# The last two groups' first FFN product made jointly by Strassen's seven block products

## The chip, the core and the metric

The kernel runs on one core of a Trainium2 chip. The metric is the device time of one execution in microseconds (us), the median over several runs. The engines of the core are TensorE (PE, matrix products into PSUM), VectorE (DVE), ScalarE (ACT), GpSimd (POOL) and SyncE (SP, which issues DMAs). In the profile PEld is TensorE's weight load, which runs beside its products.

## What is computed

Attention with squared ReLU scores for 8 batches, 12 heads, 448 rows of 64, then a Fourier mix, a normalisation and a feed-forward network (FFN) over the 3584 rows of 768:

```
scores = 1/8 * q @ k^T ; attn = relu(scores)^2 / 448 ; x = attn @ v      # heads side by side: 768 columns
u  = x + real(fft(fft(x, axis=rows), axis=columns))
un = (u - mean(u)) / sqrt(var(u) + 1e-6)                                 # over the 768 columns
out = u + relu(un @ w_ch1) @ w_ch2                                       # 768 -> 3072 -> 768
```

Only the last line concerns the change: `un @ w_ch1` is the first product, `h @ w_ch2` the second.

## The kernel before

The rows of the FFN are cut into 12 groups by `GT`: 384, 512 and 384 rows, then nine groups (numbers 3 to 11) of 256. A group's normalised rows stand transposed in SBUF as `unT`, six blocks of 128 columns of the model by up to 512 rows. Groups 2 and up get it through DRAM: `turns` issues transposing DMAs on SP (L1160) into two homes that alternate between odd and even groups, so group 11's transposes wait until TensorE has read group 9's.

**First product (`ffn`, L1446 to L1461).** For each of the 24 blocks `j` of 128 hidden columns there are six matmuls (over `m`, weights `w1_sb[m][hf]`, 128x128 each, loaded at once into SBUF), with 256 moving columns. Two blocks share one PSUM bank of the pool `BF` (two banks, `psF`), then one Relu on ACT or DVE (`relu`, L1409) writes 128x512 in bf16 to `hT`, the home of the hidden layer.

**Second product.** For groups of 256 rows it is already done by Strassen's scheme: class `Pair` takes two 128-row halves L and R of the group, even and odd blocks of the hidden layer as the inner halves, and the two column halves of `w_ch2` (384 each). `early` forms sums of hidden blocks on DVE (L1565 to L1569) in three pieces `CH` of 6, 4 and 2 block pairs, `late` one more (L1577), and `chain_a` and `chain_b` run seven products of 12 matmuls (L1583, 384 moving columns), in which a bank goes on accumulating after DVE has added what it holds so far to an output tile (`add`, L1438). The sums of the weights `T[1]` to `T[4]` are formed once, by `weight_sums` on DVE. SP loads `u` into the output tiles `o0` to `o5` and stores them (`outputs`, L1370 and L1374).

**What sets the order.** The kernel writes its own program order. Everything is a generator ("stream") that yields `need(engine, duration, deps, bufs)` and issues its instructions when it is resumed; `Streams.run` always resumes the stream whose next step could start first by its own cost estimates, with a rank to break ties:

```
LATENCY = {"PE": 0.28, "ACT": 0.18, "DVE": 0.16, "POOL": 0.2, "SP": 0.1}
def mm(n):   return n / 2400 + 0.006
def act(n):  return n / 1200 + 0.2
def dve(n):  return n / 960 + 0.15
```

`Bufs` and `Banks` are the planner's own books on which buffers are free. The real waits (semaphores) are put in by the tile framework from the tiles that instructions read and write, in the order written. PSUM has eight banks: three tiles `psS` of two banks (pool `BS`, `[128, 2, 512]` in f32, used for scores) and two tiles `psF` of one (`BF`). Each engine runs its instructions in order.

**Around the last groups.** Attention and the mix of the last batch end at about 475 us; from there on TensorE only runs FFN groups, one after the other: first product of 144 matmuls, second of 84, group 8 from 461.8 us, 9 from 491.2, 10 from 520.6, 11 from 549.9. `ffns` (L1378) runs the groups in turn.

Of the kernel before, what the change touches and what calls it, by code (L numbers as in the profile page):

```python
# [9 lines left out]
FP32 = mybir.dt.float32  # L10
# [154 lines left out]
def kernel(  # L165
# [488 lines left out]
        BX[m].free.append(e)  # L654
        x_ready[b][m].t = e

    chains = [0]

    def attention(b, left=None):

# [8 lines left out]
        while pa < NB:  # L669
# [38 lines left out]
            for part in ("scores", "values") if few else ("values", "scores"):  # L708
                if part == "values" and values:
                    held = homes.take()  # L710
                    av = held[:, 0] if homes is BS else held
                    give = lambda when, homes=homes, held=held: homes.give(held, when)
                    vn, h0 = loads[bv * NG + mv // 2][2], 2 * mv % HG
                    for c in range(4):
                        sq, _, at = sv.pop(4 * mv + c)
                        sq_ids.append((e, at))
                        for h in range(2):
                            nc.tensor.matmul(av[h * Dh:(h + 1) * Dh, 0:S], lhsT=vn[:, c, h0 + h, :],  # L718
                                             rhs=sq[:, h, :], start=(c == 0), stop=(c == 3))
                        BSQ.free.append(e)  # L720
                    av_end = e - (n * mm(S) + SWITCH if n and not few else 0.0) + LATENCY["PE"]
                    if mv % 2 == 1:
                        BQ[2].free.append(e)
                    if left is None:
# [651 lines left out]
            yield need("SP", 0.0, [e])  # L1376

    def ffns():  # L1378
        for b in range(NGR):
            yield need("SP", 0.0, [group_ready[b]])  # L1380
            yield from ffn(b)

    def ffn(b):
        T0, N, unT = groups[b]
# [24 lines left out]
        def relu(ph, e, j):  # L1409
# [18 lines left out]
            for x in ht[j:j + JN]:  # L1428
                x.t = e + LATENCY["ACT"]

        left = {(c, hf): 1 + (b > 0 and hf == 1 if c in WHOLES[b] else (c % 2, hf) != (0, 1))
                for c in range(NC) for hf in range(2)}

        def add(pc, e, c, hf, give=True):

            e = yield need("DVE", dve(DH), [e + LATENCY["PE"], ot[b, c, hf]])
            o = os[b, c, hf]
            nc.vector.tensor_tensor(o, pc[:, 0:DH], o, op=ALU.add)  # L1438
            if give:
                BF.give(pc, e)  # L1440
            left[c, hf] -= 1
            if not left[c, hf]:
                added[b, c, hf].t = e + LATENCY["DVE"]
            return e + LATENCY["DVE"]

        for j in range(0, JC, JN):  # L1446
            hf, jj = divmod(j, JC // 2)
            e = yield need("PE", 6 * JN * mm(N), [w1_ready[hf]] + ([group_ready[b]] if b > 1 else []), [BF])
            ph = BF.take()
            for i in range(JN):  # L1450
                for m in range(MC):
                    nc.tensor.matmul(ph[:, i * N:(i + 1) * N], lhsT=w1_sb[m][hf][:, (jj + i) * 128:(jj + i + 1) * 128],  # L1452
                                     rhs=unT[:, m, 0:N], start=(m == 0), stop=(m == MC - 1))
            advance(6 * JN * mm(N))
            sch.add(relu(ph, e, j), (0, 0))
            if j == JC // 2:
                ffn_begun[b].t = e
                pairs = [Pair(b, c, h, ht, add, advance) for c in PAIRS[b]]
                for p in pairs:
                    sch.add(p.early(), (0, 0.3))  # L1460
                    sch.add(p.late(), (0, 0.3))  # L1461
        if b == 0:
            unt_left.t = e
        else:
            BUNT.free.extend([e, e] if b == 2 else [e])

        for c in WHOLES[b]:
            if b > 0:
# [67 lines left out]
    class Pair:  # L1536
# [1 line left out]

        read = []

        def __init__(self, b, c, h, ht, add, advance):
            self.b, self.c, self.h, self.ht, self.add, self.advance = b, c, h, ht, add, advance
            self.L, self.R = slice(c * 128, c * 128 + 128), slice(c * 128 + 128, c * 128 + 256)
            self.ev = [slice(2 * i0, 2 * i1, 2) for i0, i1 in CH]
            self.od = [slice(2 * i0 + 1, 2 * i1, 2) for i0, i1 in CH]
            self.r12, self.r4 = ([Cell() for _ in CH] for _ in range(2))
            self.m1, self.m2, self.done = Cell(), Cell(), [Cell(), Cell()]
            self.reads = Cell(), Cell()
            self.waits, Pair.read = Pair.read, [self.reads[0], self.reads[1], *self.r4]

        def early(self):

            h, L, R_ = self.h, self.L, self.R
            if not made:
                yield need("DVE", 0.0, [un_left])
                a1 = work.tile([128, 6, 128], BF16, name="s1", tag="un2", bufs=1)
                a2 = work.tile([128, 6, 128], BF16, name="s2", tag="un3", bufs=1)
                at = JC * 256 + KP * DH
                for a, m in ((a1, upper(at, 6, 128)), (a2, upper(at + 6 * 128, 6, 128))):
                    made.append([a, m[:, 0:4], m[:, 4:6]])  # L1560
            for k, (i0, i1) in enumerate(CH):
                ev, od, s1, s2 = self.ev[k], self.od[k], made[0][k], made[1][k]
                d = dve2((i1 - i0) * 128)
                yield need("DVE", d, self.ht[2 * i0:2 * i1] + self.waits + ([upper_free] if k else []))
                nc.vector.tensor_tensor(s1, h[:, ev, R_], h[:, od, R_], op=ALU.add)  # L1565
                yield need("DVE", d)
                nc.vector.tensor_tensor(s2, s1, h[:, ev, L], op=ALU.subtract)
                e = yield need("DVE", d)
                nc.vector.tensor_tensor(h[:, ev, R_], h[:, ev, L], h[:, ev, R_], op=ALU.subtract)  # L1569
                self.r12[k].t = e + LATENCY["DVE"]  # L1570

        def late(self):

            h, L = self.h, self.L
            for k, (i0, i1) in enumerate(CH):
                e = yield need("DVE", dve2((i1 - i0) * 128), [self.m2, self.r12[k]])
                nc.vector.tensor_tensor(h[:, self.od[k], L], h[:, self.od[k], L], made[1][k], op=ALU.subtract)  # L1577
                self.r4[k].t = e + LATENCY["DVE"]

        def product(self, pc, lhs, rhs, start, i0=0, i1=KP):  # L1580

# [5 lines left out]
        def first(self, k):  # L1587

            cut = KP - 3
            yield need("PE", cut * mm(DH), self.ht[k:2 * cut:2] + [self.m1] * k, [BF])  # L1590
            pc = BF.take()
            chains[0] += 1
            self.product(pc, self.block(k, self.L), self.weights(k, 0), True, 0, cut)
            e = yield need("PE", (KP - cut) * mm(DH), self.ht[2 * cut + k::2])
            self.product(pc, self.block(k, self.L), self.weights(k, 0), True, cut)
            return pc, e

        def block(self, k, cols):

            return [self.h[:, 2 * i + k, cols] for i in range(KP)]  # L1600

        def formed(self, n):

            return [made[n][k][:, i - i0] for k, (i0, i1) in enumerate(CH) for i in range(i0, i1)]

        def weights(self, k, hf):

# [23 lines left out]
        def chain_b(self):  # L1631
# [5 lines left out]
            e = yield need("PE", d, [sums[3]] + self.r12, [BF])  # L1637
            pc = BF.take()
# [27 lines left out]
    with tc.manual_schedule():  # L1666
# [50 lines left out]
```

## Time and profile before

| | |
|---|---|
| median of 3 runs | 584.08 us (583.7 to 585.09) |
| the profiled execution, its own time | 584.67 us |
| its span, first to last instruction | 582.8 us |
| granted TensorE clock, mean | 0.997 |
| last matmul issued until | about 579.2 us |
| last output add on DVE | 579.34 to 579.90 us |

Three groups of instructions of the page that touch the change:

| group | count | mean of one |
|---|---|---|
| L1452 matmul, first product, all shapes | 1728 | 291 ns |
| L1583 matmul 128x384, second product, plain weights | 462 | 326 ns |
| L1438 add 128x384 f32 on DVE | 92 | 553 ns |

A matmul's duration in such a row includes the time in the pipeline behind the matmul before it; what a matmul costs TensorE is the distance from start to start. The span is what the profile covers; the own time of the execution is longer by what lies around it.

### The profile page before, as it was taken

Reading aid. Unit: us, or ns where it says so; the run is one execution under the profiler, and the core shown is the slowest. Engines: PE = TensorE matmul, PEld = TensorE weight load, DVE = VectorE, ACT = ScalarE, POOL = GpSimd, SP = SyncE. Lnnn points to the kernel's source line nnn. Section 1 sums busy time; section 2 is a strip of 40 time slices with the busy share of each in tenths; the row PEclk is TensorE's granted clock in tenths of the full one; section 3 lists DMA queues with packets and bytes.
Section 4 is the critical chain, followed back from the end, with each engine's and each line's share of the span. In section 5 each row is a group of like instructions: output and inputs, shape, how many; then the busy total and the mean of one; then the engine's idle time right before and its main releaser. Section 6 shows DMA issues by size and latency. Waiting matters only on the chain.

```text
span 582.8 us, 11457 instructions
## 1 busy us (share of the span) xinstructions
PE 572.9 (98%) x4476; PEld 365.7 (63%) x4476; DVE 406.4 (70%) x927; ACT 335.0 (57%) x511; POOL 133.7 (23%) x188
## 2 busy tenths in 40 slices
PE   8999999999999999999999999999999999999997
PEld 7566556544455546556857667568577786868684
DVE  5978667986669988787787878987946852222222
ACT  5866873587745787676668748777654340304040
POOL 8534021411115313421333032303300230000000
PEclk9998999999999999999999999999999999999999
DMA  9999999776947997699579987993433353031201
GB/s 120 206 211 227 222 210 134 173 131 95 181 57 189 207 172 168 116 216 167 122 123 207 180 153 147 200 176 115 126 75 100 118 151 99 30 94 36 79 30 55
DMA packets 133493, 81.85 MB, mean 140 GB/s; under 512 B 77504, under 2 KB 128704, under 8 KB 133440
## 3 DMA queue, kind: packets, MB, share of 16 engines
q0 software_dynamic: 40320, 33.63, 38.2%
q1 hardware_dynamic: 93120, 47.50, 36.3%
q8 instruction: 35, 0.57, 0.4%
q14 instruction: 18, 0.15, 0.1%
HBM read 62.91 MB, written 26.25 MB: 153 GB/s over the span
## 4 chain that ended last, share of the span: by engine, by line
PE 88%; DVE 6%; ACT 4%; issue 1%; POOL 0%; DVEq 0%; ACTq 0%; POOLq 0%
PE psF L1452 37%; PE psF L1583 26%; PE psS L736 6%; PE psF L718 5%; PE psF L1503 3%; PE psF L1477 3%; PE psS L1212 2%; ACT sq L761 2%; DVE sq L776 2%; PE psS L718 1%; PE psS L823 1%; PE psS L1026 1%; PE psS L1187 1%; PE psF L505 0%; ACT un L1087 0%
## 5 line engine op out<-in xcount | busy, mean ns | idle before, releaser
L1452 PE MATMUL psF<-unT,w 128*128 128x256 bf16 (+2 forms) x1728 | 229.8, 291 | 1.2 <-ACT unT L999 0.9
L1452 PEld LDWEIGHTS <-w 128*128 128x128 bf16 x1728 | 165.9, 98 | 61.6 <-issue 11.5
L761 ACT ACTIVATE sq<-psS 112x896 bf16<-112x896 f32 x192 | 164.4, 918 | 38.4 <-PE psS L736 38.0
L1426 ACT ACTIVATE hT<-psF 128x512 bf16<-128x512 f32 (+3 forms) x169 | 87.9, 532 | 116.6 <-PE psF L1452 115.8
L776 DVE TENSOR_TENSOR sq<-sq 112x896 bf16<-112x896 bf16 x161 | 100.6, 638 | 16.6 <-ACT sq L761 15.6
L1583 PEld LDWEIGHTS <-hT 128*128 128x128 bf16 x792 | 76.0, 98 | 54.4 <-issue 5.8
L1438 DVE TENSOR_TENSOR o<-psF,o 128x384 f32<-128x384 f32 x92 | 50.9, 553 | 44.8 <-PE psF L1583 39.6
L1583 PE MATMUL psF<-w,hT 128*128 128x384 bf16 x462 | 81.7, 326 | 0.3 <-DVE hT L1424 0.2
L736 PE MATMUL psS<-qkT 64*128 64x448 bf16 (+1 forms) x384 | 51.6, 359 | 1.2 <-ACT qkT L510 0.4
L718 PE MATMUL psF<-sq,vn 112*64 112x448 bf16 x320 | 37.9, 358 | 0.3 <-DVE o L1438 0.3
L557 DVE TENSOR_SCALAR xT<-psF 128x224 bf16<-128x224 f32 x58 | 19.8, 383 | 26.3 <-PE psF L718 26.2
L376 POOL DMA_DIRECT2D vn<-in_v_dram x24 | 17.3, 720 | 76.0 <-PE psS L736 67.7
L1059 POOL TENSOR_TENSOR u<-tp,xn 112x385 f32<-112x385 f32 (+2 forms) x14 | 13.3, 953 | 93.1 <-DVE tp L1041 81.5
L1583 PE MATMUL psF<-wsum,hT 128*128 128x384 bf16 x198 | 34.6, 326 | 0.0
L736 PEld LDWEIGHTS <-qkT 64*128 64x128 bf16 (+1 forms) x384 | 15.9, 102 | 28.7 <-issue 21.2
L376 POOL DMA_DIRECT2D qn<-in_q_dram x21 | 15.5, 739 | 69.9 <-DVE qkr L469 49.6
L718 PEld LDWEIGHTS <-vn 112*64 112x64 bf16 x384 | 17.8, 109 | 21.4 <-issue 13.7
L773 ACT ACTIVATE sq<-sq 112x896 bf16<-112x896 bf16 x31 | 29.5, 956 | 0.5
L1068 DVE BATCH_NORM_STATS2 stats<-u 112x6 f32<-112x384 f32 (+2 forms) x56 | 28.4, 541 | 0.0
L1087 ACT ACTIVATE un<-u,nmr,rstd 112x768 bf16<-112x768 f32 (+2 forms) x22 | 22.4, 1025 | 7.3 <-DVE nmr L1074 5.0
L1477 PE MATMUL psF<-w,hT 128*128 128x384 bf16 x144 | 25.1, 326 | 0.0
L1503 PE MATMUL psF<-w,hT 128*128 128x384 bf16 x144 | 24.7, 326 | 0.0
(166 smaller groups left out, 612.6 us busy)
## 6 DMA issues: line engine op xcount, KB each, us to landing
out_dram<-o SPq DMA_DIRECT2D x56, 192.0 KB, 2.2
vn<-in_v_dram POOLq DMA_DIRECT2D x24, 224.0 KB, 5.9
qn<-in_q_dram POOLq DMA_DIRECT2D x21, 224.0 KB, 5.3
kn<-in_k_dram POOLq DMA_DIRECT2D x21, 224.0 KB, 5.5
w<-in_moe_w_ch_dram POOLq DMA_DIRECT2D x12, 384.0 KB, 14.5
w<-in_moe_w_ch_dram POOLq DMA_DIRECT2D x4, 1152.0 KB, 20.5
utop<-u SPq DMA_DIRECT2D x12, 336.0 KB, 3.1
o<-utop SPq DMA_DIRECT2D x16, 192.0 KB, 3.8
```

The source lines that it names most:

```text
L376: nc.gpsimd.dma_start(out=t, in_=src[b, hs].rearrange("h (p j) d -> p h (j d)", j=4))
L718: nc.tensor.matmul(av[h * Dh:(h + 1) * Dh, 0:S], lhsT=vn[:, c, h0 + h, :], rhs=sq[:, h, :], start=(c == 0), stop=(c == 3))
L736: nc.tensor.matmul(sc[:wide, h, 0:S].rearrange("k (c q) -> k c q", c=4), lhsT=flat[ps, k0:k0 + wide], rhs=qT[ps, m % 2], start=True, stop= ...
L761: nc.scalar.activation(r, sc[:R, :, 0:S], AF.Relu)
L773: nc.scalar.activation(r, r, AF.Square)
L776: nc.vector.tensor_tensor(r, r, r, op=ALU.mult)
L1426: nc.scalar.activation(hs, ps, AF.Relu)
L1438: nc.vector.tensor_tensor(o, pc[:, 0:DH], o, op=ALU.add)
L1452: nc.tensor.matmul(ph[:, i * N:(i + 1) * N], lhsT=w1_sb[m][hf][:, (jj + i) * 128:(jj + i + 1) * 128], rhs=unT[:, m, 0:N], start=(m == 0), ...
L1477: nc.tensor.matmul(pc[:, 0:DH], lhsT=block(j, c), rhs=w2(j, hf), start=(j == 0), stop=(j == JC - 1))
L1503: nc.tensor.matmul(pc[:, 0:DH], lhsT=block(2 * i + k, c), rhs=weights[i], start=(start and i == 0), stop=(i == KP - 1), skip_group_check=True)
L1583: nc.tensor.matmul(pc[:, 0:DH], lhsT=lhs[i], rhs=rhs[i], start=(start and i == 0), stop=(i == KP - 1), skip_group_check=True)
```

## The change

Groups 10 and 11 (`ga`, `gb` in the code, `NGR - 2` and `NGR - 1`) no longer run `ffn`. Their first product is made jointly in `last_two`. Write A for group 10's rows and B for group 11's, lo and hi for the first and last three blocks `m` of the inner 768, and even and odd for the hidden blocks. The product of [A; B] with the weights is a product of 2x2 blocks; Strassen's scheme (in Winograd's form) makes it by seven block products in place of eight, with four sums of weights `S_[1..4]` and four differences of inputs `Tk[1..4]`.

- `quarter_sums` is a new stream on DVE. It forms the 24 weight sums of 128x768 (four sums, three `m`, two halves `hf`), in homes that the attention has left: the tiles of the squared scores `sq0` to `sq5`, `qkT`, `qkr`, `xT`, the folds; the third sum overwrites weights in `w1_sb` once group 9's first product is done. Then it forms the four input differences in the tables of the Fourier mix (`chan`) and in `seqm`. It begins once the last attention product is planned (`last_values`).
- `last_two` takes all three `psS` tiles and uses their halves as six banks `B6`, and four sets `BK` of three f32 copies in old homes of the mix (`u`, `qs`, `tp`, `un`, `pc`). For each of 12 rounds `i` (a pair of hidden blocks) `main` runs four products in one bank that goes on accumulating, with a copy on ACT after each of the first three and a Relu on ACT after the last; `second` and `third` run the other three in banks of their own and add a copy on DVE (`sum_out`, with a Relu in place behind it). Even the order of the rounds is left to the planner.
- The hidden layer of group 11 goes to new homes (`hB`, tiles `xn` and `vn`), and its `Pair` runs in the banks `B6`, cut into four pieces, with sums in four of the `quarter` homes. The two `Pair`s are planned together with the joint product.
- `Pair` and the output add (`adder`, moved out of `ffn`) take their pieces, homes and bank pool as arguments; for the other groups they do what they did.

The core of the diff, with the new functions:

```diff
     def ffns():
-        for b in range(NGR):
+        for b in range(NGR - 2):
             yield need("SP", 0.0, [group_ready[b]])
             yield from ffn(b)
+        yield from last_two()
...
+    def w1_part(k, m, hf):
+        return w1_sb[m][hf].rearrange("p (i o c) -> p i o c", o=2, c=128)[:, :, k]
...
+        def form(n, m, hf, x, y, op, deps=(), home=None):
+            e = yield need("DVE", dve2(6 * 128), deps)
+            if home is None:
+                home = homes.pop(0)
+            nc.vector.tensor_tensor(home, x, y, op=op)
...
+                yield from form(1, m, hf, w1_part(1, m, hf), w1_part(1, m + 3, hf), ALU.add)
+                yield from form(2, m, hf, S_[1][m, hf], w1_part(0, m, hf), ALU.subtract)
+                yield from form(4, m, hf, w1_part(0, m + 3, hf), S_[2][m, hf], ALU.subtract)
...
+                yield from form(3, m, hf, w1_part(0, m, hf), w1_part(1, m, hf), ALU.subtract, [ffn1_left],
+                                w1_part(1, m, hf))
...
+        for n, x, y in ((1, lambda: b2[:, lo], lambda: b1[:, lo]), (2, lambda: b2[:, hi], lambda: Tk[1]),
+                        (3, lambda: b2[:, hi], lambda: b2[:, lo]), (4, lambda: b1[:, hi], lambda: Tk[2])):
+            e = yield need("DVE", dve2(768), [group_ready[ga], group_ready[gb]])
+            Tk[n] = homes[n - 1]
+            nc.vector.tensor_tensor(Tk[n], x(), y(), op=ALU.subtract)
...
+    def last_two():
+        ga, gb = NGR - 2, NGR - 1
+        N = 256
+        yield need("PE", 0.0, [group_ready[ga], group_ready[gb]], [BS] * 3)
+        tiles = [BS.take() for _ in range(3)]
+        B6 = Banks(6, lambda i: tiles[i // 2][:, i % 2])
...
+        def product(ps, n, k, i, rhs, start, stop):
+            hf, ii = divmod(i, 6)
+            for m in range(3):
+                lhs = w1_part(n, m + k, hf)[:, ii] if k is not None else S_[n][m, hf][:, ii]
+                nc.tensor.matmul(ps[:, 0:N], lhsT=lhs, rhs=rhs[:, m], start=(start and m == 0),
+                                 stop=(stop and m == 2), skip_group_check=True)
+        d, half_done = 3 * mm(N), Cell()
+        def copy(ps, dst, e):
+            e = yield need("ACT", act(N), [e + LATENCY["PE"]])
+            nc.scalar.copy(dst, ps[:, 0:N])
+            return e + LATENCY["ACT"]
+        def sum_out(q, u, t, dst, deps, done, hta):
+            e = yield need("DVE", dve(N), deps, [BH[t]] if hta is not None else [])
+            nc.vector.tensor_tensor(dst, q[:, 0:N], u, op=ALU.add)
+            done(e)
+            e = yield need("DVE", 0.2)
+            nc.vector.tensor_scalar(dst, dst, 0.0, None, op0=ALU.max)
+            return e + LATENCY["DVE"]
+        def main(i):
...
+            e = yield need("PE", d, [], [B6, BK])
+            p, bk = B6.take(), BK.take()
+            product(p, 0, 0, i, b1[:, 0:3], True, False)
+            sch.add(second(i, m1, cs), (5 + 0.1 * i, 5 + 0.1 * i))
+            m1.t = e = yield from copy(p, cs[0], e)
+            e = yield need("PE", d, [e, QS[2], QT[2]])
+            product(p, 2, None, i, Tk[2], False, False)
+            e = yield from copy(p, cs[1], e)
+            e = yield need("PE", d, [e, QS[1], QT[1]])
+            product(p, 1, None, i, Tk[1], False, False)
...
+            sch.add(third(i, u4, cs, bk), (5 + 0.1 * i, 5 + 0.1 * i))
+            u4.t = e = yield from copy(p, cs[2], e)
+            e = yield need("PE", d, [e, QS[4]])
+            product(p, 4, None, i, b2[:, 3:6], False, True)
+            e = yield need("ACT", act(N), [e + LATENCY["PE"]])
+            nc.scalar.activation(at_b(0, i, i + 1, every)[:, 0], p[:, 0:N], AF.Relu)
...
+        def second(i, m1, cs):
+            e = yield need("PE", d, [], [B6])
+            r = B6.take()
+            product(r, 0, 3, i, b1[:, 3:6], True, True)
+            hta[2 * i].t = yield from sum_out(r, cs[0], 2 * i, at_a(0, i, i + 1, every)[:, 0], [e + LATENCY["PE"], m1],
+                                              lambda e: B6.give(r, e), True)
+        def third(i, u4, cs, bk):
+            e = yield need("PE", d, [QS[3], QT[3]], [B6])
+            q = B6.take()
+            product(q, 3, None, i, Tk[3], True, False)
...
+            e1 = yield need("PE", d, [gone, QT[4]])
+            product(q, 1, 3, i, Tk[4], False, True)
...
+        for i in range(KP):
+            sch.add(main(i), (5 + 0.1 * i, 5 + 0.1 * i))
...
+        pairs = [Pair(ga, 0, at_a, hta, adder(ga, 2, BF), skip, own, BF),
+                 Pair(gb, 0, at_b, htb, adder(gb, 2, B6), skip, cut, B6)]
...
+        sch.add(quarter_sums(), (6, 6))
```

In the built program TensorE has 4440 matmuls where it had 4476, DVE 102 instructions more and ACT 26 more. The order of TensorE's instructions is the same up to the first product of group 10.

More of the change, by code (lines that the diff above doesn't have):

```diff
@@ L1378, in ffns, with adder, add @@
     def ffns():
-        for b in range(NGR):
+        for b in range(NGR - 2):
             yield need("SP", 0.0, [group_ready[b]])
             yield from ffn(b)
+        yield from last_two()
+    def adder(b, NC, pool):
+        left = {(c, hf): 1 + (b > 0 and hf == 1 if c in WHOLES[b] else (c % 2, hf) != (0, 1))
+                for c in range(NC) for hf in range(2)}
+        def add(pc, e, c, hf, give=True):
+            e = yield need("DVE", dve(DH), [e + LATENCY["PE"], ot[b, c, hf]])
+            o = os[b, c, hf]
+            nc.vector.tensor_tensor(o, pc[:, 0:DH], o, op=ALU.add)
+            if give:
+                pool.give(pc, e)
+            left[c, hf] -= 1
+            if not left[c, hf]:
+                added[b, c, hf].t = e + LATENCY["DVE"]
+            return e + LATENCY["DVE"]
+        return add
@@ new lines, in last_two, with at_a, at_b, given @@
+    def last_two():
+        ga, gb = NGR - 2, NGR - 1
+        N = 256
+        yield need("PE", 0.0, [group_ready[ga], group_ready[gb]], [BS] * 3)
+        tiles = [BS.take() for _ in range(3)]
+        B6 = Banks(6, lambda i: tiles[i // 2][:, i % 2])
+        yield need("SP", 0.0, [], BU[0][1:] + BU[1][1:])
+        for x in "", "1":
+            t = work.tile([128, 3, N], FP32, name="copies", tag=f"u{x}B", bufs=1)
+            copies.append([t[:, n] for n in range(3)])
+        yield need("SP", 0.0, [], [BTS, BUN[0]])
+        ones = [work.tile([128, N], FP32, name="copies", tag=t, bufs=1)
+                for t in ("qs", "tp", "un0", "un1", f"pc{TC[0][0]}", f"pc{TC[1][0]}")]
+        copies.extend((ones[0:3], ones[3:6]))
+        BK = Banks(4, lambda i: Set(copies[i]))
+        halves = hid[0].rearrange("p j n -> p (j n)").rearrange("p (x j n) -> p x j n", x=2, n=256)
+        hA = halves[:, 0]
+        b1, b2 = groups[ga][2], groups[gb][2]
+        hta, htb = ([Cell() for _ in range(JC)] for _ in range(2))
+        def at_a(k, i0, i1, cols):
+            return hA[:, 2 * i0 + k:2 * i1:2, cols]
+        def at_b(k, i0, i1, cols):
+            for c0, c1, t in hb:
+                if c0 <= i0 < c1:
+                    assert i1 <= c1
+                    return t[:, 2 * (i0 - c0) + k:2 * (i1 - c0):2, cols]
+        every = slice(0, N)
+        def product(ps, n, k, i, rhs, start, stop):
+            hf, ii = divmod(i, 6)
+            for m in range(3):
+                lhs = w1_part(n, m + k, hf)[:, ii] if k is not None else S_[n][m, hf][:, ii]
[12 more added lines that the diff above has]
+            nc.vector.tensor_scalar(dst, dst, 0.0, None, op0=ALU.max)
+            return e + LATENCY["DVE"]
+        def main(i):
+            m1, u4 = Cell(), Cell()
+            e = yield need("PE", d, [], [B6, BK])
+            p, bk = B6.take(), BK.take()
+            cs = bk.aps
+            product(p, 0, 0, i, b1[:, 0:3], True, False)
[6 more added lines that the diff above has]
+            product(p, 1, None, i, Tk[1], False, False)
+            if i == 5:
+                half_done.t = e + LATENCY["PE"]
+            sch.add(third(i, u4, cs, bk), (5 + 0.1 * i, 5 + 0.1 * i))
[4 more added lines that the diff above has]
+            nc.scalar.activation(at_b(0, i, i + 1, every)[:, 0], p[:, 0:N], AF.Relu)
+            B6.give(p, e)
+            htb[2 * i].t = e + LATENCY["ACT"]
+        def second(i, m1, cs):
[8 more added lines that the diff above has]
+            product(q, 3, None, i, Tk[3], True, False)
+            gone = Cell()
+            def given(e):
+                gone.t = e + LATENCY["DVE"]
+            def first():
+                htb[2 * i + 1].t = yield from sum_out(q, cs[2], None, at_b(1, i, i + 1, every)[:, 0],
+                                                      [e + LATENCY["PE"], u4], given, None)
+            sch.add(first(), (0, 0))
+            e1 = yield need("PE", d, [gone, QT[4]])
+            product(q, 1, 3, i, Tk[4], False, True)
+            def leave(e):
+                B6.give(q, e)
+                BK.give(bk, e)
+            hta[2 * i + 1].t = yield from sum_out(q, cs[1], 2 * i + 1, at_a(1, i, i + 1, every)[:, 0],
+                                                  [e1 + LATENCY["PE"]], leave, True)
+        ffn_begun[ga].t = ffn_begun[gb].t = sch.engine["PE"]
+        for i in range(KP):
+            sch.add(main(i), (5 + 0.1 * i, 5 + 0.1 * i))
+        skip = lambda us: None
+        own = [(k, i0, i1) for k, (i0, i1) in enumerate(CH)]
+        cut = [(k, max(i0, c0), min(i1, c1)) for k, (i0, i1) in enumerate(CH) for c0, c1, _ in hb
+               if max(i0, c0) < min(i1, c1)]
+        pairs = [Pair(ga, 0, at_a, hta, adder(ga, 2, BF), skip, own, BF),
+                 Pair(gb, 0, at_b, htb, adder(gb, 2, B6), skip, cut, B6)]
+        own_sums = [S_[n][m, 0] for n, m in ((1, 0), (1, 1), (2, 0), (2, 1))]
+        pairs[1].waits = [half_done, pairs[0].r12[0]]
+        pairs[1].sums = lambda n, i0, i1: own_sums[2 * n + i0 // 6][:, i0 % 6:i0 % 6 + i1 - i0]
+        for n, p in enumerate(pairs):
+            sch.add(p.early(), (0, 7 + n))
+            sch.add(p.late(), (0, 7 + n))
+            sch.add(p.chain_a(), (7 + 1 * n, 0))
+            sch.add(p.chain_b(), (6.9 + 1 * n, 0))
+        yield need("SP", 0.0, pairs[1].done)
@@ L1429, in relu @@
                 x.t = e + LATENCY["ACT"]
[L1431 to L1444, printed above, removed]
+        add = adder(b, NC, BF)
         for j in range(0, JC, JN):
@@ L1568, in early @@
                 e = yield need("DVE", d)
[L1569 to L1570 removed]
+                nc.vector.tensor_tensor(at(0, i0, i1, R_), at(0, i0, i1, L), at(0, i0, i1, R_), op=ALU.subtract)
+                self.r12[x].t = e + LATENCY["DVE"]
         def late(self):
[L1574 to L1578, printed above, removed]
+            at, L = self.at, self.L
@@ new lines, in late, with sums @@
+            for x, (k, i0, i1) in enumerate(self.pieces):
+                e = yield need("DVE", dve2((i1 - i0) * 128), [self.m2, self.r12[x]])
+                nc.vector.tensor_tensor(at(1, i0, i1, L), at(1, i0, i1, L),
+                                        self.sums(1, i0, i1), op=ALU.subtract)
+                self.r4[x].t = e + LATENCY["DVE"]
+        def sums(self, n, i0, i1):
+            k = [c0 <= i0 < c1 for c0, c1 in CH].index(True)
+            return made[n][k][:, i0 - CH[k][0]:i1 - CH[k][0]]
@@ L1598, in block @@
         def block(self, k, cols):
-            return [self.h[:, 2 * i + k, cols] for i in range(KP)]
+            return [self.at(k, i, i + 1, cols)[:, 0] for i in range(KP)]
         def formed(self, n):
-            return [made[n][k][:, i - i0] for k, (i0, i1) in enumerate(CH) for i in range(i0, i1)]
+            return [self.sums(n, i, i + 1)[:, 0] for i in range(KP)]
         def weights(self, k, hf):
@@ L1636, in chain_b @@
             yield from self.add(pc, e, c, 0)
-            e = yield need("PE", d, [sums[3]] + self.r12, [BF])
-            pc = BF.take()
+            e = yield need("PE", d, [sums[3]] + self.r12, [self.pool])
+            pc = self.pool.take()
             self.product(pc, self.block(0, self.R), T[3], True)
```

77 lines of the change are left out of this document (61 added, 16 removed).

## The prediction

> **What bounds the kernel now.** I read the page's engine table first, then the chain of waits in order of time, then the timeline of the last 120 us engine by engine.
>
> ```profile
> PE 572.9 (98%) x4476; PEld 365.7 (63%) x4476; DVE 406.4 (70%) x927; ACT 335.0 (57%) x511; POOL 133.7 (23%) x188
> ...
> 520.56 15.72 PE psF L1452 x144
> 536.28 13.65 PE psF L1583 x84
> 549.93 15.72 PE psF L1452 x144
> 565.65 13.66 PE psF L1583 x84
> ```
>
> The last two groups are four blocks of TensorE work end to end, with nothing between them. A first-product matmul takes 15.72/144 = 0.1092 us, so one over a 128x256 tile pays 288 x 0.1092 = 31.45 us for the two groups that the change touches. Only TensorE time counts here, and any wait of TensorE is paid in full. The other engines are nearly idle in this stage: the page's 40 slices give DVE 2 tenths in the last seven, ACT 0 to 4.
>
> What one handover costs (TensorE ends, another engine reads PSUM, TensorE goes on) can be read from the timeline:
>
> ```profile
> 520.40 15.88 PE L1452 MATMUL psF<-unT,w 128*128 128x256 bf16 x144
> 521.96 0.60 ACT L1426 ACTIVATE hT<-psF 128x512 bf16<-128x512 f32 x1 [14.35 <-PE psF L1452]
> 477.38 4.06 PE L1583 MATMUL psF<-w,hT 128*128 128x384 bf16 x24
> 479.53 0.56 DVE L1438 TENSOR_TENSOR o<-psF,o 128x384 f32<-128x384 f32 x1 [0.50 <-PE psF L1583]
> 124.51 0.66 ACT L999 CAST unT<-psS 128x582 bf16<-128x582 f32 x1
> 125.22 0.59 PE L1452 MATMUL psF<-unT,w 128*128 128x512 bf16 x2 [0.92 <-ACT unT L999]
> ```
>
> Twelve matmuls from 520.40 are issued by 521.71 and ACT starts at 521.96: 0.25. Twelve of 0.1626 (13.66/84) from 477.38 end at 479.33 and DVE starts at 479.53: 0.20. ACT ends at 125.17 and TensorE starts at 125.22: 0.05. The rows by shape give the reads:
>
> ```profile
> L1426 ACT ACTIVATE hT<-psF 128x256 bf16<-128x256 f32 x18 | 6.9, 385 | 5.4 <-PE psF L1452 5.1
> L1424 DVE TENSOR_SCALAR hT<-psF 128x256 bf16<-128x256 f32 x6 | 2.5, 420 | 1.2 <-PE psF L1452 1.2
> L333 DVE TENSOR_SCALAR channeg<-chan 128x386 bf16<-128x386 bf16 x3 | 0.8, 259 | 0.4 <-ACT chan L310 0.4
> ```
>
> So a handover over ACT is 0.25 + 0.385 + 0.05 = 0.685 us, over DVE 0.20 + 0.42 + 0.05 = 0.67. In the old kernel six matmuls per bank half and twelve per bank (1.31 us) stand between two uses, so nothing is felt.
>
> **The change part by part.**
>
> *Removed:* 288 matmuls (31.45 us, all on the path) and 24 Relus of 128x512 on ACT (0.60 each, beside TensorE).
>
> *Added on TensorE:* 12 rounds of 7 products of 3 matmuls, 252 x 0.1092 = 27.52 us. The gain before any wait is 31.45 - 27.52 = **3.93 us**. The second product's 168 matmuls of 0.1626 stay.
>
> *Added weight sums:* 24 DVE adds of 128x768 and four of the inputs, at the 0.55 of the early sums of the pair (L1565 to L1569, 0.55 to 0.56). Eighteen stand between 448 and 479 us, 18 x 0.47 (step from start to start) = 8.5 us, where DVE's idle times add up to 9.4 (2.65, 0.30, 0.29, 0.85, 0.65, 0.20, 2.73, 1.24, 0.50); also two DVE Relus of 0.69 there go to ACT. They queue ahead of the early sums of group 8's pair, which ended at 479.02 and are needed by the matmul at 481.28: 2.3 us of cover, so nothing. Six more overwrite weights after group 9's last first-product matmul (506.75) and push one output add by about 0.45, needed only at 510.65 and over at 509.9: nothing. The four input differences wait for group 11's transposes, issued at 506.94 and 508.16, landing in at most 3.5 us, ahead of their place in DVE's queue (513.4). TensorE's order up to 520.40 is unchanged in the built program, and no bank wait there was close (0.4 us left at each psF). I take 0 for all of this, bounds 0 and 2 (the overflow of 8.5 over 9.4 if the sums cannot use the small gaps).
>
> *Moved DMAs:* SP's loads of group 11's outputs stand some 30 us earlier; the one that reuses a slot (store of group 10's first block, 2.2 us to landing, then a load, 3.6) is ready about 15 us after the second product begins, when DVE reaches its add. By this estimate DVE waits at most 0.3 there, and behind it stands an add that TensorE releases 1 us later. Zero.
>
> *Added waits, the heart of it.* The joint stage takes the three two-bank psS tiles and uses their halves as six banks. Per round there are four ACT reads and three DVE sums (each with a Relu in place behind it, 0.23 by L333's row). The planner knows a wait only per half. In the built program the waits follow the whole tile: of the 59 waits of TensorE on a psS tile in this stage, 35 are for ACT or DVE reading the *other* half, and ACT and DVE wait for matmuls and for each other across halves too. So a tile is a queue: product, read, product, read. With a product of 3 x 0.1092 = 0.33, the next product in a tile waits 0.68 less 0.33 for each product placed between: 0.68, 0.36 or 0.03 for none, one or two.
>
> I walked the 84 products in the built order with these durations. The start: four products fill both halves of tiles 0 and 1 by 1.31. The copy of the first starts at 0.66 + 0.25 = 0.91, after the *second* product, and ends at 1.29; the DVE sum of the other half runs from 1.32 to 1.74; so the fifth product, into the half that was copied, starts at 1.79 and not 1.31: 0.48 lost. Going on so gives 23 waits: 0.48, 0.48, 0.81, 0.36, 0.36, 0.34, 0.26, 0.15, 0.33, 0.15, 0.26, 0.26, 0.36, 0.77, 0.03, 0.34, 0.15, 0.34, 0.61, 0.02, 0.15, 0.35, 0.36, together **7.7 us**. The same walk with each half waiting only for itself gives none. If every handover is 0.1 cheaper the sum is 5.8, if 0.1 dearer 9.8; these are the bounds (the trace's two PSUM readers differ by 0.05 in their start, and the sum and copies from f32 to f32 are not in it; L876's f32 copy of 128x384 at 0.474 against 0.490 says no dearer).
>
> *Sum:* -3.93 + 7.7 = **+3.8 us**, bounds +1.9 and +5.9. The profiled execution took 584.67 (span 582.8 and 1.87 around it): 588.4. It lies 0.6 above the median of the runs, 584.08, so a median of **587.9**, own range 586.0 to 590.0.
>
> The Trainium skill ("PSUM — Partial Sum Buffer", section on bank collisions) says that accesses of PSUM need guarding by bank and quadrant. By that rule the waits across halves, which are different banks, guard against nothing; the program has them all the same, and the sum by the rule is the first rival's. No row shown here tests it.
>
> **The rivals.**
>
> 1. *The waits across halves cost nothing, as planned.* For: the walk with separate halves, no wait at all; the planner allows more for a handover than I measure. Against: the waits stand in the program. It decides where a handover costs under 0.48 us: there the waits equal the 3.93 saved. Time: 584.08 - 3.9 = 580.2 at best. DVE would then be close to the bound: 36 sums of 0.42 + 0.03 + 0.14 are 21 us, and about 6 of pair sums, against 27.5.
>
> 2. *The clock drops.* With 7.7 us of waits in 35, TensorE works 78% of the stage, about 68% from 7 to 10 us into it. The trace has one drop:
>
> ```profile
> 11.40:14.80 3.40, 2.97 (x54) 2.49 (x54) 2.62 (x6) 3.17 (x5) 2.40 (x7) 1.00 1.43 189
> ...
> 50.50:53.90 3.40, 2.07 (x35) 1.44 (x35) 2.92 (x6) 3.27 (x6) 1.69 (x2) 1.00 1.13 252
> 53.90:57.30 3.40, 3.40 (x26) 1.63 (x24) 2.54 (x5) 1.22 (x2) 0.00 (x0) 0.50 1.26 209
> ```
>
> (TensorE's busy time is the second number, the granted clock the third from the end.) 2.07 busy of 3.40 was followed by 3.4 us at half clock, 2.97 was not. The stage lies between. One drop halves 3.4 us of matmuls, up to 1.7 us, less what the waits absorb; one to three give 589 to 593. The Trainium skill ("TensorE: Matmul & The Clock Gate", section on the second HAM failure mode) tells of short idle times between matmul groups from cycling PSUM that make the clock swing; the trace shows only the one drop above.
>
> 3. *The sums come late.* If DVE's 18 adds overflow the gaps, the pair of group 8 starts late at 481.28, by up to 2 us: 588 to 590.
>
> 4. *Waits and gain cancel*: handovers near 0.48, 584 within its 0.3%.
>
> **How the numbers follow.** Chances: the forecast 0.75, clock 0.08, late sums 0.05, cancelling 0.05, waits free 0.07. A difference of 0.3% (1.75 us) is about what a measurement tells from none. Faster by more: 0.07 (rival 1). Within: 0.05. Slower: 0.88. The range 585.6 to 590.8 holds the forecast's own bounds, the late sums and part of the clock case, and leaves out rival 1 and the worst of rival 2.
>
> **What would show it.** Right: the last 62 us have TensorE idle before the joint products by 0.3 to 0.8 at a time, released by DVE sums and ACT copies of the other half, 7 to 8 us in all and none before 520; 252 matmuls at 0.109; second product unbroken at 0.163. Wrong: waits summing under 4 us (handover mis-sized), idle TensorE before 520 (late sums), or a granted clock below 1 in the stage.

## The result and the profile after

| | before | after |
|---|---|---|
| median of 6 runs each | 584.52 us (583.7 to 585.24) | 588.19 us (586.93 to 589.92) |
| ratio, 95% interval | | 1.006 [1.0041, 1.0079] |
| the profiled execution, its own time | 584.67 us | 589.04 us |
| its span | 582.8 us | 587.3 us |
| granted TensorE clock, mean | 0.997 | 0.996 |

The joint first product makes the kernel 0.6% slower, by 3.67 us between the medians. The page's engine table and the chain of waits in order of time, of the changed kernel (start, length, what):

```profile
PE 571.9 (97%) x4435; PEld 361.9 (62%) x4440; DVE 439.4 (75%) x1029; ACT 338.9 (58%) x537; POOL 135.1 (23%) x188
```

```profile
462.86 15.72 PE psF L1662 x144
478.58 13.77 PE psF L1801 x84
492.35 15.72 PE psF L1662 x144
508.07 13.65 PE psF L1801 x84
521.72 0.67 PE psS L1506 x6
522.41 0.38 ACT copies L1513
522.82 0.43 DVE hT L1518
523.29 1.49 PE psS L1506 x12
...
562.31 9.75 PE psF L1801 x60
572.06 11.71 PE psS L1801 x72
```

TensorE has 36 matmuls fewer (4476 and 4435 are recorded; some records are missing), and yet the end is later. Where before there were four blocks of TensorE end to end, the chain now runs through ACT and DVE from the start of the joint stage on: product, copy on ACT, sum on DVE, product. Group 8's first product in the chain of the kernel before is

```profile
461.82 15.72 PE psF L1452 x144
```

so from its start to the end of the last matmul it was 565.65 + 13.66 - 461.82 = 117.49 us before; now it is 572.06 + 11.71 - 462.86 = 120.91: **+3.42 us**. This stretch is the sharp measure of this study. Group 8 itself begins 1.04 us later in this execution (462.86 against 461.82), behind work whose order on TensorE the change did not touch; in the profiles of this study group 8 began anywhere from 459.87 to 463.28 us. The first of the new sums stand ahead of group 8, at 449.3, and delay nothing there: from the matmul 400 places ahead of group 8's first one it is 53.04 us in both profiles.

How much TensorE waits is best read from the starts. Its timeline, changed kernel (start, length, engine, line, what; idle time before, with what ended it):

```profile
521.56 1.47 PE L1506 MATMUL psS<-unT,w 128*128 128x256 bf16 x12
523.29 0.49 PE L1506 MATMUL psS<-chan,quarter 128*128 128x256 bf16 x3 [0.26 <-DVE hT L1518]
...
524.93 0.49 PE L1506 MATMUL psS<-chan,w 128*128 128x256 bf16 x3
525.69 0.81 PE L1506 MATMUL psS<-chan,quarter 128*128 128x256 bf16 x6 [0.26 <-DVE hT L1518]
...
526.99 0.49 PE L1506 MATMUL psS<-sumx,w 128*128 128x256 bf16 x3
528.08 0.49 PE L1506 MATMUL psS<-unT,quarter 128*128 128x256 bf16 x3 [0.59 <-DVE hB L1518]
```

Twelve matmuls of 0.1092 from 521.56 are over at 522.87, but the thirteenth starts at 523.29: 0.42 lost. The row says 0.26 idle, since it counts the last matmul busy for its whole row (1.47 us for twelve of 0.1092), 0.16 beyond the time at which the next could have started. The same way 525.69 - 524.93 - 0.33 = 0.43 and 528.08 - 526.99 - 0.33 = 0.76. Summed over the joint stage, start to start less the matmuls' own time, TensorE waits **7.19 us**; the profile's table of waits names only 3.2 of them:

```profile
PE psS L1506 <- DVE hB L1518: 1.6, 5, 0.6
PE psS L1506 <- DVE hT L1518: 1.0, 4, 0.3
PE psS L1506 <- ACT hB L1545: 0.4, 1, 0.4
PE psS L1506 <- ACT copies L1513: 0.2, 1, 0.2
```

The sum closes: -3.93 (36 matmuls fewer) + 7.19 + 0.12 (just before group 8's second product, below) = +3.38, against +3.42 measured. What stands in the handovers, by shape (busy time in us, mean of one in ns, idle time before them and what ended it):

```profile
L1513 ACT COPY copies<-psS 128x256 f32<-128x256 f32 x36 | 12.9, 373 | 26.1 <-PE psS L1506 23.1 <-DVE hB L1518 1.7 <-DVE hT L1518 1.0
L1518 DVE TENSOR_TENSOR hT<-psS,copies 128x256 bf16<-128x256 f32 x24 | 9.9, 422 | 7.6 <-ACT copies L1513 4.6 <-PE psS L1506 2.3 <-ACT hB L1545 0.7
L1521 DVE TENSOR_SCALAR hT<-hT 128x256 bf16<-128x256 bf16 x24 | 5.1, 225 | 0.6
L1545 ACT ACTIVATE hB<-psS 128x256 bf16<-128x256 f32 x12 | 4.6, 385 | 7.6 <-PE psS L1506 7.6
```

One copy takes 373 ns, one sum 422, its Relu 225, the Relu on ACT 385: close to the 385 and 420 that the prediction took. From 521.5 to 559.7 ACT is busy for 17.2 us and DVE for 26.6 of 38.2, so neither is full.

### The profile page after: what moved, and what is told of

The parts are those of the page before. It is cut to its first block, busy times and chain, and to the rows that moved or that the text cites. A ratio compares the mean times of both kernels' runs of the same rounds, so it can differ in the third digit from the quotient of the medians.

```text
span 587.3 us, 11522 instructions
## 1 busy us (share of the span) xinstructions
PE 571.9 (97%) x4435; PEld 361.9 (62%) x4440; DVE 439.4 (75%) x1029; ACT 338.9 (58%) x537; POOL 135.1 (23%) x188
## 4 chain that ended last, share of the span: by engine, by line
PE 79%; DVE 9%; ACT 5%; DMA 3%; SPq 2%; issue 1%; POOL 0%; DVEq 0%; ACTq 0%; POOLq 0%
PE psF L1662 29%; PE psF L1801 20%; PE psS L738 5%; PE psF L718 4%; PE psS L1506 3%; PE psF L1690 3%; PE psF L1716 3%; ACT sq L763 3%; PE psS L1214 2%; PE psS L1801 2%; DVE sq L778 2%; DMA qkT<-qkr 2%; PE psS L718 1%; DMA ntop<-un 1%; SPq L652 1%
## 5 line engine op out<-in xcount | busy, mean ns | idle before, releaser
L1662 PE MATMUL psF<-unT,w 128*128 128x256 bf16 (+2 forms) x1435 | 198.3, 295 | 2.6 <-ACT unT L1001 0.9
L1662 PEld LDWEIGHTS <-w 128*128 128x128 bf16 x1440 | 138.0, 98 | 59.4 <-issue 12.8
L1649 ACT ACTIVATE hT<-psF 128x512 bf16<-128x512 f32 (+3 forms) x147 | 74.7, 521 | 69.7 <-PE psF L1662 67.2
L1801 PEld LDWEIGHTS <-hT 128*128 128x128 bf16 x720 | 69.0, 98 | 49.8 <-issue 6.1
L1801 PE MATMUL psF<-w,hT 128*128 128x384 bf16 x420 | 74.7, 326 | 0.3 <-DVE hT L1647 0.2
L1395 DVE TENSOR_TENSOR o<-psF,o 128x384 f32<-128x384 f32 x85 | 47.0, 553 | 31.6 <-PE psF L1801 26.2
L1801 PE MATMUL psF<-wsum,hT 128*128 128x384 bf16 x180 | 31.6, 326 | 0.0
L1513 ACT COPY copies<-psS 128x256 f32<-128x256 f32 x36 | 12.9, 373 | 26.1 <-PE psS L1506 23.1
L1690 PE MATMUL psF<-w,hT 128*128 128x384 bf16 x144 | 25.1, 326 | 0.0
```

What stands on the lines that cost most here:

```text
L1649: nc.scalar.activation(hs, ps, AF.Relu)
L1690: nc.tensor.matmul(pc[:, 0:DH], lhsT=block(j, c), rhs=w2(j, hf), start=(j == 0), stop=(j == JC - 1))
L1801: nc.tensor.matmul(pc[:, 0:DH], lhsT=lhs[i], rhs=rhs[i], start=(start and i == 0), stop=(i == KP - 1), skip_group_check=True)
```

## The experiments

All of them at once, the medians beside those of the kernel before on the same chip; "stretch" is from group 8's first matmul to the end of the last, "waits" TensorE's in the joint stage from start to start, both from the profiled execution of each:

| kernel | median us | before | ratio, 95% interval | stretch us | waits us |
|---|---|---|---|---|---|
| before | | 584.52 | | 117.49 | |
| changed | 588.19 | 584.52 | 1.006 [1.0041, 1.0079] | 120.91 | 7.19 |
| tiles of their own, six | 580.65 | 584.41 | 0.9924 [0.9902, 0.9947] | 113.67 | 0.0 |
| tiles of their own, four | 582.50 | 584.99 | 0.9951 [0.9935, 0.9967] | 113.83 | 0.12 |
| sums alone | 584.94 | 584.41 | 1.0004 [0.9987, 1.0021] | 117.60 | none |
| three banks | 584.96 | 584.41 | 1.0005 [0.9982, 1.0027] | 117.40 | 3.70 |
| other partner | 586.79 | 584.41 | 1.0044 [1.0025, 1.0062] | 120.00 | 6.30 |
| flat tile | 587.70 | 584.99 | 1.0064 [1.004, 1.0089] | 120.90 | 7.19 |
| short reads | 583.16 | 584.68 | 0.9977 [0.9955, 0.9999] | 116.14 | 2.43 |
| double copy | 593.03 | 584.68 | 1.0146 [1.0125, 1.0166] | 127.11 | 13.40 |
| own tiles, double copy | 583.16 | 584.68 | 0.9969 [0.9941, 0.9996] | 115.97 | 2.28 |

In every row with joint products, 117.49 - 3.93 + 0.11 + waits gives the stretch within 0.05 us. Both sides are read from the same starts, so this says where the time went and not why; nothing else in the stretch moved.

**Tiles of their own.** Before the joint stage the pool of the three two-bank tiles is closed, and six one-bank tiles are taken in the same place; the order of instructions on every engine is that of the changed kernel.

```
-        tiles = [BS.take() for _ in range(3)]
-        B6 = Banks(6, lambda i: tiles[i // 2][:, i % 2])
+        pairs_pool.__exit__(None, None, None)
+        psum6 = ctx.enter_context(tc.psum_pool(name="ps6", bufs=1))
+        B6 = Banks(6, lambda i: psum6.tile([128, 512], FP32, name="psG", tag=f"G{i}", bufs=1))
```

> The joint stage with six one-bank PSUM tiles of their own in place of the halves of three two-bank tiles; every engine's instruction order is that of the changed kernel, only the waits differ. Theory (waits across the halves of a tile are what costs): nearly all of the 7.2 us of TensorE's waits in the joint stage go, the matmuls saved (3.93 us) are left, 584.5 - 3.9 = 580.6, between 580.0 and 581.5. Rival 1 (ACT and DVE, or two engines at neighbouring banks, are the limit, however the tiles are tracked): the waits stay, 586.5 to 588.5. Rival 2 (the weight sums or something else ahead of the stage costs 1 us or more of the 3.7): 582 to 583.

Measured: 580.65 us, 0.9924 [0.9902, 0.9947] of the kernel before. The timeline of TensorE and the chain at the same products as above:

```profile
521.96 1.47 PE L1509 MATMUL psG<-unT,w 128*128 128x256 bf16 x12
523.27 0.49 PE L1509 MATMUL psG<-chan,quarter 128*128 128x256 bf16 x3
...
524.91 0.49 PE L1509 MATMUL psG<-chan,w 128*128 128x256 bf16 x3
525.24 0.82 PE L1509 MATMUL psG<-chan,quarter 128*128 128x256 bf16 x6
```

```profile
508.47 13.65 PE psF L1804 x84
522.12 25.54 PE psG L1509 x234
547.67 1.46 PE psF L1804 x9
```

523.27 - 521.96 = 12 x 0.1092: no wait. 234 matmuls take 25.54 us, 0.1091 each. The same order of the same instructions in the same PSUM, with waits only where a bank itself is read, runs without a gap. So the waits across halves are the whole of the loss in the joint stage; rival 1 of this expectation (the engines are the limit) falls, and rival 2 too: of the 3.93 us saved, 3.82 arrive in the stretch (117.49 - 113.67) and 3.76 in the medians. This version beats both kernels. TensorE has waits of its own across halves, and ACT and DVE have them too; which of them cost more was not taken apart.

The copies run beside the products at the length that they had in the changed kernel:

```profile
L1516 ACT COPY copies<-psG 128x256 f32<-128x256 f32 x35 | 12.6, 373 | 22.0 <-DMA out_dram<-o 13.3 <-PE psG L1509 8.4 <-DVE hT L1524 0.3
```

**The sums alone.** `ffns` runs all twelve groups by `ffn`, and the last six sums go to the homes of the hidden halves:

```
-        for b in range(NGR - 2):
+        for b in range(NGR):
...
-        yield from last_two()
...
-                                w1_part(1, m, hf))
+                                own.pop())
```

> All 24 weight sums and the four input differences are formed at their places, but the last two groups run their own first products as before, so nothing reads the sums; the last six stand in the homes of the hidden halves instead of over the weights. Theory (sums are hidden): 584.5, within 0.6 of before. Rival (they delay the pair of group 8 or an output add): 585.5 to 587.

Measured: 584.94 against 584.41, an interval that holds no change. The stretch is 0.11 longer than before. That tenth can be placed: ahead of group 8's second product the profile of the changed kernel has, on ACT,

```profile
476.98 1.03 ACT L1089 ACTIVATE un<-u,nmr,rstd 112x768 bf16<-112x768 f32 x1 [0.38 <-DVE nmr L1076]
477.91 1.30 ACT L1649 ACTIVATE hT<-psF 128x512 bf16<-128x512 f32 x2
```

and TensorE's second product starts at 478.54, where the first product's last matmul from 477.76 (six of 0.1092) would let it start at 478.42. The sums filled DVE, so two Relus moved to ACT, one stands behind a normalisation there, and the bank is free 0.12 later.

**Three banks.** `B6 = Banks(3, lambda i: tiles[i][:, 0])`: one half of each tile, so that the planner's books agree with the waits.

> Only the first half of each two-bank tile is used: three banks instead of six, but now no bank shares its tile, and the planned order knows every wait. Theory (sharing, not the number of banks, is what costs): walking the products in the order built for three banks gives 3.1 us of waits against 3.93 saved in the one place, and after its second-product chains +0.8 in all against before, so 584.5 + 0.8 = 585.3, between 584.3 and 586.5: faster than the changed kernel though it has half the banks. Rival (the stage lacks banks): more waits than with six, over 588.5.

Measured: 584.96, and 3.70 us of waits where the +0.8 of the walk stands for 4.7 in all (the 3.1 of the expectation is about its part before the second product begins). With half the banks the stretch is 3.5 us shorter than with six shared ones. The rival falls, though three banks still cost 3.70 us of waits that six tiles of their own do not.

**Other partner.** `B6 = Banks(6, lambda i: tiles[i % 3][:, i // 3])`.

> The same six halves in the same planned order, but bank i has bank i+3 as the other half of its tile instead of its neighbour. Theory: the same walk with the other partners gives 1.4 us less of waits: 588.2 - 1.4 = 586.8, between 586.0 and 587.6. Rival (waits do not come from partners): no change, 588.2.

Measured: 586.79; waits 6.30, which is what the walk's own sums give (7.7 - 1.4), and 0.9 less than the changed kernel's. The order and the reads are the same; only who shares a tile changed, and the stretch followed (120.00 against 120.91). The medians lie 1.40 apart, as forecast, but only 0.9 of that is in the stretch, so the close match is partly chance.

**Flat tile.** The three tiles as `[128, 1024]`, viewed as two halves.

> The changed kernel with the three PSUM tiles declared as one row of 1024 columns and then viewed as two halves, where they were declared as two halves of 512. Theory (the unit that is waited for is the tile, whatever its shape): the same waits, 588.2, between 587 and 589.5. Rival (the declared shape with its two halves blurs the ranges, and a flat tile is told apart by columns): 580.6.

Measured: 587.70, waits 7.19 as in the changed kernel. The shape in which a tile is declared is no remedy; the unit that is waited for is the tile.

**Short reads.** `copy`, `sum_out` (with its Relu in place) and the Relu of `main` are cut to 64 columns, and POOL sets group 11's hidden blocks to zero ahead; the other 192 columns are left out of the result. For example

```
-            nc.scalar.copy(dst, ps[:, 0:N])
+            nc.scalar.copy(dst[:, 0:64], ps[:, 0:64])
```

> The changed kernel with shared tiles, but each PSUM read of the joint stage (copy, sum, Relu) covers only 64 of its 256 columns; the other 192 columns of the hidden halves are left out (set to zero ahead). TensorE's work and every order stay. Theory (the waits are handovers through shared tiles, so they shrink with the reads): a copy handover falls by 192/1200 = 0.16 us, a sum by 192/960 = 0.20, to 0.47 to 0.52; the walk of the products gives 2.8 us of waits in place of 7.2, so 588.2 - 4.4 = 583.8, between 583 and 585. Rival (the waits are a fixed cost of signalling between the engines): 0.5 us of change at most, 587.5 to 588.5.

Measured: 583.16, waits 2.43. The copy's row and the sum's are now

```profile
L1516 ACT COPY copies<-psS 128x64 f32<-128x64 f32 x36 | 7.5, 213 | 28.2 <-PE psS L1509 25.5 <-DVE hB L1521 1.3 <-DVE hT L1521 0.9
L1521 DVE TENSOR_TENSOR hT<-psS,copies 128x64 bf16<-128x64 f32 x24 | 5.3, 224 | 9.0 <-ACT copies L1516 4.2 <-PE psS L1509 4.1 <-ACT hB L1548 0.6
```

The copy takes 0.213 us where it took 0.373, 0.16 less; the sum 0.224 where it took 0.422, 0.20 less; and the waits fall by 4.76. A fixed cost of signalling would have left the waits as they were; two thirds of them go with the length of the reads.

**Double copy**, with shared tiles: the line `nc.scalar.copy(dst, ps[:, 0:N])` stands twice.

> The changed kernel with each of the 36 copies made twice in a row on ACT. Theory: the copy stands inside the handovers of the shared tiles, so about 0.3 us more in each; the walk gives 6.8 us more waits: 588.2 + 6.8 = 595.0, between 593.5 and 596.5. Rival (ACT's own time is beside TensorE's and is mostly hidden): 588 to 590.

Measured: 593.03, waits 13.40, 6.2 more (the walk said 6.8). In the medians it is 4.8 more than the changed kernel's, below the range given. The stretch is 6.2 longer, as the waits say, so the rest lies ahead of group 8: in its profiled execution group 8 begins 2.99 us earlier than in the changed kernel's (459.87 against 462.86). The clock drop of the last section is a small part of it: two of the changed kernel's six runs had it and none of these four, and the changed kernel's four runs without it have a median of 587.89, which leaves 5.1. What else differs ahead of group 8 stays open.

**Double copy, tiles of their own.** The same line twice, in the version with six one-bank tiles.

> The version with six tiles of their own, with each copy made twice. Theory: with each bank waiting only for itself, much of the dearer handover is hidden behind products in other banks: the walk gives 3.2 us of waits where the single copy had none, 580.65 + 3.2 = 583.9, between 582.5 and 585, under half of what the same edit costs with shared tiles. Rival (a dearer copy costs the same however the banks are tracked): 580.65 + 6.8 = 587.5.

Measured: 583.16, waits 2.28. The same 36 extra copies cost 2.3 us with tiles of their own and 6.2 with shared ones. Even with its copies doubled, the version with its own tiles is faster than the kernel before.

**Four tiles of their own.** As the first experiment, with `Banks(4, ...)`.

> The version with tiles of their own, but with four one-bank tiles in place of six (the plan is made anew for four). Theory (a bank that waits only for itself is what counts, the number of banks little): the walk gives 0.2 us of waits, 580.65 + 0.2 = 580.8, between 580 and 582, seven below the shared six. Rival (three banks fell behind six separate ones by 4.3 us because banks are short, evenly with their number): about a third to half of that at four, 582 to 583.

Measured: 0.12 us of waits, a stretch of 113.83: in the stage four banks do what six do, and the theory holds there. The median, 582.50, lies above the range given (582) and in the rival's. The profile does not bear the rival out: the gaps of its TensorE in the joint stage add up to 0.12 us, and its stretch is 0.16 longer than with six tiles, where the medians lie 1.85 apart. Where the rest comes from is not shown (the last section comes back to it).

## Why the prediction was right

The forecast was 587.9 us, and 588.19 was measured. That the two lie 0.3 apart is partly chance: the waits came out 0.5 us smaller than forecast and the sums 0.11 dearer, and the sum started from 584.08, the median of three runs of the kernel before, where the six runs beside the changed kernel have 584.52. The difference, forecast as +3.8, was 3.67 between the medians and 3.42 in the stretch. The mechanism is the one that was forecast. By its steps:

- *The gain of 3.93 us before any wait:* right. With the waits gone, 3.82 of it arrive in the stretch, and the 0.11 that is missing is the price of the sums.
- *The handover of 0.685 over ACT and 0.67 over DVE:* right as a mean, with each off by some 0.06. In the changed kernel three matmuls start at 528.08, the last is issued by 528.41, ACT starts at 528.60 and TensorE at 529.04: 0.19 + 0.39 + 0.05 = 0.63. Over DVE, three from 530.31 are issued by 530.64, the sum starts at 530.91, takes 0.42, and 0.05 follow: 0.74.

```profile
528.08 0.50 PE psS L1506 x3
528.60 0.39 ACT hB L1545
529.04 0.83 PE psS L1506 x6
529.89 0.38 ACT copies L1513
530.31 0.50 PE psS L1506 x3
530.91 0.44 DVE hB L1518
```

- *Waits of 7.7 us, bounds 5.8 and 9.8, the first of them 0.48, 0.48, 0.81:* 7.19, the first of them 0.42, 0.43, 0.76. The mechanism is right and the size 7% high. Short reads and double copies show that the sum follows the handover, other partners that it follows the sharing.
- *The same walk with separate halves gives none:* right, as measured with tiles of their own.
- *The break-even at a handover of 0.48 us:* too low. With short reads the handovers are some 0.18 shorter than the 0.68 of the mean above, about 0.50, and the waits are 2.43, well under 3.93. On a straight line between 2.43 at 0.50 and 7.19 at 0.68, an estimate from two points, they are 3.93 at about 0.56. The waits grow by some 26 us for 1 us of handover, against 20 between the prediction's bounds.
- *Nothing for the weight sums:* 0.11 us, shown alone. "no bank wait there was close" was the wrong part: a Relu moved to ACT frees its bank 0.12 too late. The six sums over the weights and the four of the inputs cost nothing: from group 8's second product to the joint stage TensorE has no wait.
- *Nothing for the moved DMAs:* right. From 562.31 to 583.77 TensorE runs without a gap, (9.75 + 11.71)/132 = 0.1626 a matmul, so no output add was late enough to hold a bank.
- *Second product unbroken:* nearly; one wait of 0.30 at 559.71, where it takes a bank whose tile ACT still reads. It is in the 7.19.
- *Rival 1, waits across halves free:* wrong for this kernel, and the true course as soon as each bank is its own tile: 580.2 was its time, 580.65 is that version's. The Trainium skill ("PSUM — Partial Sum Buffer", section on bank collisions) asks for guarding by bank, and by that rule the waits across halves guard against nothing. The version with its own tiles agrees: TensorE, ACT and DVE work in different banks at once, at full speed (0.1091 us a matmul, 373 ns a copy).
- *Rival 2, the clock:* it stays at 1.00 through the stage, and windows with hardly more work than the 2.07 us of the prediction's row have no drop. Even double copies, which leave TensorE 2.2 to 3.1 us of work in each 3.4, do not lower it (columns: window, length, busy time of TensorE, its weight loads, DVE, ACT and POOL with counts, granted clock, DMA share, GB/s):

```profile
522.00:525.40 3.40, 2.21 (x19) 1.66 (x18) 1.30 (x4) 2.69 (x9) 0.00 (x0) 1.00 0.49 158
525.40:528.80 3.40, 2.26 (x20) 1.72 (x19) 1.45 (x5) 1.42 (x4) 0.00 (x0) 1.00 0.15 47
528.80:532.20 3.40, 2.43 (x19) 1.67 (x18) 1.81 (x7) 2.00 (x6) 0.00 (x0) 1.00 0.00 0
```

- *Rival 3, sums late by up to 2 us:* 0.11. *Rival 4, cancelling:* the three-bank version is that case, at 584.96.

## What to carry to other kernels

When several small jobs share a PSUM tile, count what the program waits for, not what the plan believes: here a tile was the unit of waiting, and six halves of three tiles were worth less than three banks. Give each bank that is handed over on its own a tile of its own, above all where a product (0.33 us) is shorter than a handover (0.63 to 0.74); the same order of instructions went from 0.6% slower to 0.8% faster that way. A saving on the bounding engine that needs more handovers is priced by walking the products through the waits that the program has, and starts should be compared with starts, since the idle time that is listed falls short (here 3.2 of 7.19 us).

## What the runs showed of the hardware

The clock drop in the attention's part (the prediction read it as the answer to a window with 2.07 us of TensorE work) comes in some executions and not in others, at nearly the same load. The version with four tiles and the one with six have 2.40 and 2.39 us of work in the window from 50.50 to 53.90; in the former the granted clock is 0.92 in that window already and 0.58 in the next:

```profile
50.50:53.90 3.40, 2.40 (x35) 1.53 (x36) 2.92 (x7) 3.22 (x6) 1.35 (x2) 0.92 1.14 251
53.90:57.30 3.40, 3.40 (x27) 1.60 (x26) 2.35 (x4) 1.02 (x2) 0.00 (x0) 0.58 1.25 207
```

In the latter it is 1.00 in both:

```profile
50.50:53.90 3.40, 2.39 (x36) 1.64 (x37) 2.92 (x7) 3.24 (x6) 1.36 (x2) 1.00 1.14 254
53.90:57.30 3.40, 3.40 (x35) 1.85 (x33) 3.31 (x4) 2.48 (x3) 0.00 (x0) 1.00 1.24 205
```

Four of the eleven profiles have this drop (before, changed, other partner, four tiles; the flat tiles, with 2.15 us of work in that window, do not), and they are the four with a mean clock of 0.996 or 0.997. By that mark 13 of the 58 runs of the kernel before that stood beside the experiments had it, with a median of 585.75 us; the 30 at 1.000 have 584.31. So some 1.4 us of the scatter between runs goes with this one drop, as much as some of the differences studied here. What decides whether it comes is open.

The drop alone does not explain the 1.85 us between the medians with four and with six tiles, though four of the six runs with four tiles had it and only one of the six with six: that one took 580.51, below the median of its kernel, and the two runs with four tiles without it took 580.65 and 583.04. The kernel before was itself 0.58 slower beside the four tiles (584.99 against 584.41). The rest of that difference is open.
